# Attention and mixer: zero products around q's transposes, 1e-6 on TensorE, and a new order of the early loads

## The chip, the cores and the metric

The kernel runs on one core of a Trainium2 chip. Its time is the device time of one execution in microseconds, here the median over several runs. The engines of the core run side by side and each works through its own list of instructions in order: TensorE (PE) multiplies matrices, with weight loads shown apart as PEld; VectorE (DVE) and ScalarE (ACT) work element by element; GpSimd (POOL) casts, fills and issues transfers; SyncE (SP) issues transfers.

## The reference

Eight batches of eight heads, 576 positions, 64 features a head. First an attention without softmax, whose features are weighted by cosine and sine of the position; then a mixer on its output, laid out as x of 576 positions by 512 channels.

```python
theta = np.pi / 2.0 * pos / S
q_p = phi(q, cos_w, sin_w)          # [relu(q) * cos, relu(q) * sin]
k_p = phi(k, cos_w, sin_w)
kv = np.einsum('bhsf,bhsd->bhfd', k_p, v)
z = np.sum(k_p, axis=2)
num = np.einsum('bhsf,bhfd->bhsd', q_p, kv)
den = np.einsum('bhsf,bhf->bhs', q_p, z)[..., None] + 1e-06
x = num / den                       # heads side by side
h = x.transpose(0, 2, 1) @ U @ V    # U: 576 x 32, V: 32 x 576
u = x + h.transpose(0, 2, 1)
out = u + np.maximum(u @ w_ch1, 0.0) @ w_ch2   # 512 -> 2048 -> 512
```

## The kernel before

A batch's 576 positions are cut into four chunks of 128 rows and a tail of 64 (chunk number 4). Two batches make a pair, whose tails share one chunk. All matrix work is in bf16 with sums in fp32.

**The first batch** is done on its own and in a hurry. SP issues the loads of q, k and the second half of v's heads (the odd rows and the even rows apart: load_odd, load_even). POOL issues U and V, then v's first half of heads (load_v0, after cast_v's three casts), then the quarters of w_ch1 (w1_load: 512 of the 2048 columns each). PE meanwhile multiplies zeros (keep_warm: n products of 512 columns and `short` of 128), until q_prep has made a chunk's features; then it transposes q chunk by chunk, with one more zero product behind each. After four more zero products come spread_v (V's transposed layout), the z products of k, and kv0_mm, which needs v's first half. first_chain then carries batch 0 to the first products of the mixer: den_mm multiplies q by z, recip adds 1e-6 and takes the reciprocal on DVE, xh_mm and xh_norm make x, A_mm and the uTd functions make u transposed, and g_half begins the products with w_ch1.

**From there on** PE's order is written out as a list of slots. A slot is one piece of PE work of four matmuls or more: slots 0 to 15 are u times w_ch1 for batch 0 (g1_main, line 572, evicted by ACT at line 581), 16 to 31 the products with w_ch2 for batch 0 (g2_part, line 744; slots 16 to 19 use w_ch2's first quarter, the next four its second), and slot 32 begins batch 1's g1_main. Beside a slot, `at(j, ...)` hangs the small work of batch 1's attention: it is put into every engine's list just behind slot j. In the order of need these units are:

- q_prep and k_prep: for one chunk, the cosine half and the sine half, each on the engine named in the pair (DVE is V_, ACT is A_)
- qtr_unit: eight transposes of q on PE, evicted by DVE
- v_prep: a cast of one chunk of v for half of the heads
- kv_unit: k times v for half of the heads, 20 products (line 343)
- x_two and x_unit: x of one chunk, with 1e-6 and the reciprocal on DVE and the scaling on ACT or DVE
- A_unit, u_mm, u_add, utr_dma: the mixer's first part and the transposes by SP

The list of `at` is filled chunk by chunk in the order (4, 0, 1, 2, 3). So behind a slot that has several units, they stand in that order: at slot 12 of the kernel before, DVE's list has the casts of v's chunks 4, 0, 1 and 2, then k's chunk 3, then v's chunk 3.

**The queues.** A transfer is issued by the engine in whose list it stands, in order, when what it waits for is done. SP's list after batch 0's loads: q of batch 1 (line 94 and 88), k, then v in four pieces; after slot 15 a tiny transfer into `mark2` that waits for w_ch2's first quarter (the function gate, line 1240), the transposes of u of batch 0 (u_dma), a second gate for w_ch2's second quarter, and the loads of batch 2. POOL's list: after w_ch1's first two quarters a tiny copy into `mark` that waits for batch 0's k features, then the other two quarters; then a copy into `mark` that waits for batch 1's k (line 1227), and w_ch2's four quarters.

Of the kernel before, what the change touches and what calls it, by code (L numbers as in the profile page):

```python
# [11 lines left out]
BF16 = mybir.dt.bfloat16  # L12
# [5 lines left out]
def kernel(  # L18
# [22 lines left out]
    NJ = DH // P  # L41
    NPAIR = B // 2
    TS = 64

    def tail(b):
        lo = TS * (b % 2)  # L50
# [76 lines left out]
    def cast(eng, o, i):  # L127
        if eng is nc.scalar:
            nc.scalar.activation(out=o, in_=i, func=AF.Copy, bias=0.0, scale=1.0)
        else:  # L130
            eng.tensor_copy(out=o, in_=i)  # L131
# [89 lines left out]
    V_.memset(v_ext[:, 0:4, :, D:E], 1.0)  # L221
    V_.memset(q_tlT, 0.0)
    V_.memset(x_tl, 0.0)

    def keep_warm(n, tag, bufs, short=0):
        w_ps = ps.tile([P, 512], FP32, tag=tag, bufs=bufs, name="w_ps")
        for i in range(n + short):
            w = 512 if i < n else P
            nc.tensor.matmul(  # L229
                out=w_ps[:, 0:w], lhsT=zero[:, 0:P], rhs=zero[:, 0:w], start=True, stop=True  # L230
            )
# [11 lines left out]
        G_.memset(v_ext[:, 4 + i, :, :], 0.0)  # L243
        G_.memset(v_ext[tail(i), 4 + i, :, D:E], 1.0)

    def cast_v():
        nine_v = stV.rearrange("r (m k) -> r k m", k=9)
        for i in range(2):
            cast(
                G_,  # L250
                V_nat[:, 0:512].rearrange("r (c m i) -> r c m i", c=4, i=2)[:, :, :, i],
                nine_v[:, 5 * i : 5 * i + 4, :],
            )
        cast(G_, V_nat[:, 512:S], nine_v[:, 4, :])

    def cast_u():
        cast(G_, U_bf[:, 0:4, :], stU[:, 0:4, :])
# [149 lines left out]
    def recip(rec, den):  # L407
        nc.vector.tensor_scalar(out=rec, in0=den, scalar1=1e-6, scalar2=None, op0=ALU.add)
        nc.vector.reciprocal(out=rec, in_=rec)
# [641 lines left out]
    O2, G3 = ("o", 2), ("g", 3)  # L1051

    def den_mm(b, h0, h1, d_ps):
        for c in range(5):
            for h in range(h0, h1):
                nc.tensor.matmul(
                    out=d_ps[:, c, h - h0 : h - h0 + 1],
                    lhsT=qT_of(b, c, h),
                    rhs=z_sb[:, h : h + 1],
                    start=True,  # L1060
                    stop=True,
                )

    def xh_mm(b, c, h0, tag=None, bufs=None, acc=None):
# [48 lines left out]
    def first_chain(b):  # L1113
        v_block(b, 4, 8, 3, 4, A_)
        v_prep(b, 4, 8, (4,), (A_,))
        v_block(b, 4, 8, 0, 3, V_)
        cast(A_, z_sb, z_ps)
        cast(V_, kv_sb[b][:, 0:4, 0:D], kv_lo)
        spread_evac(A_)
        d0 = ps.tile([P, 2, 512], FP32, tag="X", bufs=1, name="d_ps")  # L1120
        d = [d0[:, i, 0:20].rearrange("p (c h) -> p c h", h=4) for i in range(2)]
        rec = [pool.tile([P, 5, 4], FP32, tag="rec5", bufs=2, name="rec5") for _ in (0, 1)]
        den_mm(b, 0, 4, d[0])
        recip(rec[0], d[0])
        x0 = [xh_mm(b, c, 0, *G3) for c in ORD[0:3]]
        for n in (0, 1):
            xh_norm(b, ORD[n], 0, rec[0], x0[n])
        kv_unit(b, 1, *O2, A_, D)
        for c, tg in zip(ORD[3:], (O2, T1)):
            x0.append(xh_mm(b, c, 0, *tg))  # L1130
        den_mm(b, 4, 8, d[1])
        xh_scale(b, ORD[3], 0, rec[0], x0[3])
        xh_norm(b, ORD[2], 0, rec[0], x0[2])
        recip(rec[1], d[1])
        xh_norm(b, ORD[4], 0, rec[0], x0[4])
        x1 = [xh_mm(b, c, 4, *G3) for c in ORD[0:2]]
        a_ps = ps.tile([P, DM], FP32, tag="o", bufs=2, name="a_ps")
        for _ in range(2):
            nc.tensor.matmul(out=a_ps, lhsT=zero[:, 0:P], rhs=zero, start=True, stop=True)
        x1.append(xh_mm(b, ORD[2], 4, *G3))  # L1140
        x34 = ps.tile([P, 2, 512], FP32, tag="X", bufs=1, name="x34_ps")
        for i in range(2):
            x1.append(x34[:, i, 0:256].rearrange("p (i d) -> p i d", d=D))
            xh_mm(b, ORD[3 + i], 4, acc=x1[-1])
        A_mm(b, a_ps, (0, 1))
        xh_scale(b, ORD[2], 4, rec[1], x1[2])
        for n in (0, 1):
            xh_norm(b, ORD[n], 4, rec[1], x1[n])
        cast(V_, A_of(b)[0:TS, :], a_ps[0:TS, 0:P])
        uT_alloc(b)  # L1150
        for i, (tag, bufs) in enumerate((T1, O2)):
            uT_ps[b, i] = ps.tile([P, 4, P], FP32, tag=tag, bufs=bufs, name="uT_ps")
            open_mm(b, i, uT_ps[b, i], range(4))
        for i in range(2):
            uTd_mm(b, i)
        uTd_evac(b, 0, A_)
        for n in (3, 4):
            xh_norm(b, ORD[n], 4, rec[1], x1[n])
        uTd_evac(b, 1, V_)
        A_mm(b, a_ps, (2, 3))  # L1160
        cast(A_, A_of(b)[TS:P, :], a_ps[TS:P, 0:P])
        u2 = ps.tile([P, 2, 512], FP32, tag="X", bufs=1, name="u2")
        uT_ps[b, 2] = u2[:, 0, :].rearrange("p (c t) -> p c t", c=4)
        uT_ps[b, 3] = ps.tile([P, 4, P], FP32, tag="T", bufs=1, name="uT_ps")
        for i in (2, 3):
            open_mm(b, i, uT_ps[b, i], range(4))
        for i in (2, 3):
            uTd_mm(b, i)
        uTd_evac(b, 2, V_)
        uTd_evac(b, 3, A_)  # L1170
        for d in range(2):
            g_half(b, d, range(3))
        for d in range(2):
            g_half(b, d, (3,), O2)

    FEATS = [(V_, V_ if c == 3 else A_) for c in TL]
    qT_alloc(0)
    keep_warm(4, "X", 1, 72)
    t_q = []
    for c in TL:  # L1180
        tg = G3 if c < 3 else O2
# [1 line left out]
    for c in TL:  # L1183
        q_prep(0, c, FEATS[c])
        qtr_mm(0, c, 0, H, t_q[c])
        keep_warm(1, "X", 1)
    for c, eng in zip(TL, (V_, A_, V_, A_, V_)):
        qtr_evac(0, c, eng, t_q[c])
    keep_warm(4, "X", 1)
    cast_v()  # L1190
    load_v0()
    for n in range(2):
        w1_load(n)
    cast_u()
# [24 lines left out]
    first_chain(0)  # L1219
    load_odd(qst, q, 1)  # L1220
    load_even(qst, q, 1)
    load_odd(kst, k, 1)
    load_even(kst, k, 1)
    for h0 in (0, 4):
        load_odd(vst, v, 1, h0, h0 + 4)
        load_even(vst, v, 1, h0, h0 + 4)
    G_.tensor_copy(out=mark, in_=kst[0:TS, 7, 4, 0:1])
    for n in range(4):
        w2_load(n)
    q_prep(1, 4, (V_, A_))  # L1230
    q_prep(1, 0, (V_, V_))


# [8 lines left out]
    for n, c in enumerate(ORD):  # L1242
        if n > 1:
            at(n - 2, lambda c=c: q_prep(1, c, (V_, V_)))
        tg = ("T", 1) if n % 2 else O2
        at((1, 2, 4, 5, 6)[n], lambda c=c, tg=tg: qtr_unit(1, c, eng=V_, tag=tg[0], bufs=tg[1]))
        at((6, 7, 9, 10, 12)[n], lambda c=c: k_prep(1, c, (V_, A_)))
        for i in range(2):
            at((12, 14)[i], lambda c=c, i=i: v_prep(1, 4 * i, 4 * i + 4, (c,), (V_,)))
    for hg in range(2):  # L1250
        at((14, 16)[hg], lambda hg=hg: kv_unit(1, hg, "T", 1))

    side = {}

# [33 lines left out]
                op=ALU.mult,  # L1288
            )

    for a, c in ((17, 0), (17, 4), (19, 1), (19, 2), (20, 3)):
        if c in (0, 2):
            at(a, lambda c=c: x_two(1, c))
        else:
            at(a, lambda c=c: x_unit(1, c, "X", 1))
# [190 lines left out]
```

## Time and profile before

| what | us |
|---|---|
| median of 3 runs (295.07 to 295.89) | 295.85 |
| the profiled execution | 295.75 |
| its span, from first to last instruction | 294.0 |
| PE busy | 288.3 |
| DVE busy | 205.7 |
| ACT busy | 161.7 |
| POOL busy | 51.0 |
| first transpose of q starts on PE | 8.94 |
| first product of kv0_mm starts | 16.16 |
| first product of den_mm starts | 17.17 |
| first product with w_ch1 starts | 23.18 |
| first product with w_ch2 starts (slot 16) | 40.44 |

Landings of the early transfers in that execution, from the issue to the last of the engines that carry it:

| transfer | issued | landed |
|---|---|---|
| k of batch 0, even rows | 3.06 | 12.10 |
| v of batch 0, first half, even rows | 8.37 | 16.11 |
| w_ch1, first and second quarter | 9.13, 9.87 | 20.47, 24.92 |
| q of batch 1, even rows | 10.21 | 23.83 |
| w_ch1, third and fourth quarter | 15.76, 16.50 | 30.86, 34.94 |
| k of batch 1, odd and even rows | 14.97, 15.68 | 28.09, 32.83 |
| v of batch 1, four pieces | 16.33 to 24.68 | 35.12 to 37.31 |
| w_ch2, four quarters | 33.41 to 35.83 | 39.93, 43.10, 45.95, 49.16 |

How to read it: a busy engine is not yet the bound, and a transfer that lands late costs only what an engine in PE's chain waits for it. The profile lists an engine's idle time in brackets with what ended it. The ends of matmuls are modelled; the steps from one end to the next are what PE's stream is read by.

### The profile page before, as it was taken

The numbers are of one execution on the slowest core, as the hardware profiler recorded it, in microseconds if no ns is written. First come the engines' busy times: TensorE is split into PE (matmuls) and PEld (weight loads), VectorE is DVE, ScalarE is ACT, GpSimd is POOL, SyncE is SP. The second block draws the span as 40 slices with busy tenths as digits, with TensorE's granted clock in tenths as the row PEclk, the third lists the DMA queues.
The fourth block names the chain that finished last, engine by engine and source line by source line (L and its number), as shares of the span: only waits on it lengthen the run. The fifth ranks groups of instructions, "written<-read, shape, count | busy, mean of one in ns | idle before, by whom it ended". The sixth has DMA issues, their size and how long they took to land.

```text
span 294.0 us, 7234 instructions
## 1 busy us (share of the span) xinstructions
PE 288.3 (98%) x2922; PEld 194.9 (66%) x2922; DVE 205.7 (70%) x497; ACT 161.7 (55%) x323; POOL 51.0 (17%) x89
## 2 busy tenths in 40 slices
PE   8999999999999999999999999999999999999995
PEld 6775454445745545676757666766776668889984
DVE  4878645696774569837736794678747798785864
ACT  2856654066791767568735865378752334446220
POOL 8520400012020002310500231021200100000240
PEclk9999999999999999999999999999999999999999
DMA  7999999999997998999599939992900141101013
GB/s 218 297 254 252 242 188 221 217 308 211 330 197 101 280 283 221 216 320 308 136 189 222 308 101 236 224 353 65 240 13 3 74 89 74 71 2 71 2 72 145
DMA packets 90709, 54.07 MB, mean 184 GB/s; under 512 B 58420, under 2 KB 87380, under 8 KB 90676
## 3 DMA queue, kind: packets, MB, share of 16 engines
q1 hardware_dynamic: 84116, 43.85, 59.7%
q0 software_dynamic: 6416, 9.63, 14.6%
q8 instruction: 23, 0.38, 0.5%
q10 hardware_dynamic: 144, 0.13, 0.1%
q14 instruction: 10, 0.08, 0.1%
HBM read 36.86 MB, written 9.44 MB: 157 GB/s over the span
## 4 chain that ended last, share of the span: by engine, by line
PE 89%; DMA 6%; ACT 2%; DVE 1%; issue 1%; DVEq 0%; ACTq 0%
PE g_ps L572 30%; PE h_ps L873 27%; PE o_ps L744 10%; DMA kst<-in_k_dram 6%; PE gt_ps L706 5%; PE c_ps L666 4%; PE kv_ps L343 3%; PE w_ps L229 3%; PE x_ps L418 3%; PE h_ps L744 1%; PE a_ps L441 1%; ACT k_p L302 1%; PE va_ps L471 1%; PE t_ps L373 1%; PE x_ps L1266 0%
## 5 line engine op out<-in xcount | busy, mean ns | idle before, releaser
L572 PE MATMUL g_ps<-uT,w_bf 128*128 128x512 bf16 x440 | 107.5, 379 | 0.1
L581 ACT ACTIVATE hid<-g_ps 128x512 bf16<-128x512 f32 x112 | 66.2, 599 | 72.3 <-PE g_ps L572 72.1
L572 PEld LDWEIGHTS <-w_bf 128*128 128x128 bf16 x440 | 41.3, 98 | 37.3 <-issue 0.8
L873 PEld LDWEIGHTS <-hid 128*128 128x128 bf16 x480 | 45.4, 98 | 9.6
L873 PE MATMUL h_ps<-w_bf,hid 128*128 128x256 bf16 x288 | 37.0, 273 | 0.0
L831 DVE TENSOR_TENSOR o_sb<-u_bf,h_ps 128x256 f32<-128x256 bf16 x44 | 18.3, 415 | 18.1 <-PE h_ps L873 17.9
L744 PE MATMUL o_ps<-w_bf,hid 128*128 128x512 bf16 x128 | 30.1, 379 | 0.0
L131 POOL CAST v_ext<-vst 128x512 bf16<-128x512 f32 (+1 forms) x26 | 18.5, 734 | 54.8 <-DMA vst<-in_v_dram 53.6
L873 PE MATMUL h_ps<-w_s,S 128*128 128x256 bf16 x208 | 26.5, 272 | 0.0
L873 PE MATMUL h_ps<-w_s,hid 128*128 128x256 bf16 x192 | 24.9, 273 | 0.0
L931 POOL DMA_DIRECT2D out_dram<-o_sb x16 | 10.0, 625 | 84.2 <-DVE o_sb L831 81.4
L479 DVE TENSOR_TENSOR u_bf<-x_bf,va_ps 128x512 bf16<-128x512 bf16 x27 | 17.7, 680 | 7.7 <-PE va_ps L471 5.4
L873 PEld LDWEIGHTS <-S 128*128 128x128 bf16 x208 | 19.9, 98 | 4.4
L831 DVE TENSOR_TENSOR o_sb<-o_sb,h_ps 128x256 f32<-128x256 f32 (+1 forms) x36 | 15.4, 430 | 10.4 <-PE h_ps L873 10.2
L744 PEld LDWEIGHTS <-hid 128*128 128x128 bf16 x128 | 11.6, 98 | 12.5
L706 PE MATMUL gt_ps<-uT_tl,w_bf 128*128 128x128 bf16 x256 | 16.1, 219 | 0.0
L428 DVE TENSOR_TENSOR x_bf<-x_ps,rec 128x512 bf16<-128x512 f32 x22 | 15.2, 691 | 0.8
L706 PEld LDWEIGHTS <-w_bf 128*128 128x128 bf16 x256 | 15.0, 98 | 1.0
L302 ACT ACTIVATE k_p<-kst,cosw 128x512 bf16<-128x512 f32 x20 | 14.2, 712 | 0.1
L302 ACT ACTIVATE q_p<-qst,sinw 128x512 bf16<-128x512 f32 x18 | 12.6, 709 | 1.9 <-DMA qst<-in_q_dram 1.9
L604 DVE TENSOR_TENSOR hid<-kept,c_ps 128x256 bf16<-128x256 f32 x24 | 9.4, 417 | 5.3 <-PE c_ps L666 2.8
L229 PE MATMUL w_ps<-zero 128*128 128x128 bf16 (+1 forms) x86 | 11.2, 301 | 1.2 <-DVE zero L140 1.2
(186 smaller groups left out, 419.5 us busy)
## 6 DMA issues: line engine op xcount, KB each, us to landing
qst<-in_q_dram SPq DMA_DIRECT2D x14, 512.0 KB, 6.0
kst<-in_k_dram SPq DMA_DIRECT2D x14, 512.0 KB, 6.4
vst<-in_v_dram SPq DMA_DIRECT2D x12, 512.0 KB, 6.7
out_dram<-o_sb POOLq DMA_DIRECT2D x19, 256.0 KB, 3.9
w_bf<-in_moe_w_ch_dram POOLq DMA_DIRECT2D x8, 512.0 KB, 12.3
out_dram<-o_sb SPq DMA_DIRECT2D x16, 256.0 KB, 2.8
qst<-in_q_dram SPq DMA_DIRECT2D x2, 640.0 KB, 13.6
kst<-in_k_dram SPq DMA_DIRECT2D x2, 640.0 KB, 9.0
```

The lines of the kernel that those rows point to most:

```text
L131: eng.tensor_copy(out=o, in_=i)
L229: nc.tensor.matmul(out=w_ps[:, 0:w], lhsT=zero[:, 0:P], rhs=zero[:, 0:w], start=True, stop=True)
L302: nc.scalar.activation(out=o, in_=i, func=AF.Relu, bias=0.0, scale=w)
L428: nc.vector.tensor_tensor(out=x_of(b, c, rows).rearrange("p (g i d) -> p g i d", g=2, d=D), in0=view[:, :, :, 0:D], in1=rec[rows].unsqueez ...
L479: nc.vector.tensor_tensor(out=u_bf[b][:, j, :, :], in0=x_bf[b][:, :, ns], in1=va[b][j].rearrange("p (c n) -> p c n", c=4), op=ALU.add,)
L572: nc.tensor.matmul(out=g_ps.rearrange("p (c t) -> p c t", c=4), lhsT=w1_bf[:, d, j * P : j * P + P], rhs=uT[b][:, d, :, :], start=(d == 0) ...
L581: nc.scalar.activation(out=hid[b][:, j, :], in_=g_ps, func=AF.Relu, bias=0.0, scale=1.0)
L666: nc.tensor.matmul(out=w[to].rearrange("p (c t) -> p c t", c=2), lhsT=lhs[:, d, cs], rhs=rhs[:, d], start=(first and d == 0), stop=(d == 1 ...
L706: nc.tensor.matmul(out=g_ps[:, jj, :], lhsT=w1_bf[:, d, j * P : j * P + P], rhs=uT_tl[pr][:, d, :], start=(d == 0), stop=(d == 3),)
L744: nc.tensor.matmul(out=o[:, cols], lhsT=lhs[:, j, c * P : c * P + P], rhs=w2_bf[:, j, cols], start=(j == 0), stop=(j == NJ - 1),)
L831: eng.tensor_tensor(out=o, in0=x, in1=y, op=ALU.add)
L873: nc.tensor.matmul(out=acc, lhsT=lhs[:, j, :], rhs=rhs[:, j, :], start=(j == 0 and at is not None), stop=(j == 7), skip_group_check=at is ...
```

## The change

Five edits, all before slot 24:

- keep_warm at the start: 4 products of 512 columns and 72 of 128 become 13 and 10; the one zero product behind each chunk's transposes goes (five in all); the four behind the evictions become eight.
- cast_v is cut in two: the first cast stands ahead of load_v0, the other two behind it.
- den_mm begins with two products of one row, of 20 columns each, that put 1e-6 into the whole bank (the sum of 9.98e-07 and 1.62e-09 in bf16, times 1); the den products then add to it, and first_chain takes the reciprocal without the add on DVE. Three memsets on DVE fill the operand. x_unit and x_two keep recip.
- SP's loads of batch 1's k and v stand behind a tiny transfer into mark2 that waits for w_ch1's second quarter. POOL's copy into mark, with w_ch2's loads behind it, waits no longer for batch 1's k but for batch 1's q features of chunk 1.
- The units of batch 1 come later: transposes of q from slots 1, 2, 4, 5, 6 to 4, 5, 7, 8, 9; k_prep from 6, 7, 9, 10, 12 to 11 to 15; v_prep from 12 and 14 to 14 and 15; kv_unit from 14 and 16 to 16 and 17; the x units from 17, 17, 19, 19, 20 to 18, 18, 20, 20, 21. The sine half of q's chunk 4 and of k's chunks 0 and 2 moves from ACT to DVE.

```diff
+    EPS = (9.98377799987793e-07, 1.622538547962904e-09, 1.0)
...
+    eps = pool.tile([1, 2 * P + 20], BF16, tag="S2", bufs=2, name="eps")
+    for cs, part in zip((slice(0, P), slice(P, 2 * P), slice(2 * P, None)), EPS):
+        V_.memset(eps[:, cs], part)
...
-    def cast_v():
+    def cast_v(i):
         nine_v = stV.rearrange("r (m k) -> r k m", k=9)
-        for i in range(2):
-            cast(
...
+        cast(
...
+        if i:
+            cast(G_, V_nat[:, 512:S], nine_v[:, 4, :])
...
     def den_mm(b, h0, h1, d_ps):
+        for i in range(2):
+            nc.tensor.matmul(
+                out=d_ps.rearrange("p c h -> p (c h)"), lhsT=eps[:, i * P : i * P + P],
+                rhs=eps[:, 2 * P :], start=(i == 0), stop=(i == 1),
+            )
...
-                    start=True,
+                    start=False,
                     stop=True,
+                    skip_group_check=True,
...
-        recip(rec[0], d[0])
+        V_.reciprocal(out=rec[0], in_=d[0])
...
-        recip(rec[1], d[1])
+        V_.reciprocal(out=rec[1], in_=d[1])
...
-    keep_warm(4, "X", 1, 72)
+    keep_warm(13, "X", 1, 10)
...
         qtr_mm(0, c, 0, H, t_q[c])
-        keep_warm(1, "X", 1)
...
-    keep_warm(4, "X", 1)
-    cast_v()
+    keep_warm(8, "X", 1)
+    cast_v(0)
     load_v0()
+    cast_v(1)
...
     load_even(qst, q, 1)
+    nc.sync.dma_start(out=mark2, in_=w1_bf[0:1, 0, 512:513])
     load_odd(kst, k, 1)
...
-    G_.tensor_copy(out=mark, in_=kst[0:TS, 7, 4, 0:1])
-    for n in range(4):
-        w2_load(n)
-    q_prep(1, 4, (V_, A_))
+    q_prep(1, 4, (V_, V_))
     q_prep(1, 0, (V_, V_))
...
-        at((1, 2, 4, 5, 6)[n], lambda c=c, tg=tg: qtr_unit(1, c, eng=V_, tag=tg[0], bufs=tg[1]))
-        at((6, 7, 9, 10, 12)[n], lambda c=c: k_prep(1, c, (V_, A_)))
+        at((4, 5, 7, 8, 9)[n], lambda c=c, tg=tg: qtr_unit(1, c, eng=V_, tag=tg[0], bufs=tg[1]))
+        at((11, 12, 13, 14, 15)[n], lambda c=c, n=n: k_prep(1, c, (V_, V_ if n % 2 else A_)))
         for i in range(2):
-            at((12, 14)[i], lambda c=c, i=i: v_prep(1, 4 * i, 4 * i + 4, (c,), (V_,)))
+            at((14, 15)[i], lambda c=c, i=i: v_prep(1, 4 * i, 4 * i + 4, (c,), (V_,)))
     for hg in range(2):
-        at((14, 16)[hg], lambda hg=hg: kv_unit(1, hg, "T", 1))
+        at((16, 17)[hg], lambda hg=hg: kv_unit(1, hg, "T", 1))
+
+    def w2_loads():
+        G_.tensor_copy(out=mark, in_=q_p[1][0:TS, 1, 7, 127:128])
+        for n in range(4):
+            w2_load(n)
+
+    at(3, w2_loads)
...
-    for a, c in ((17, 0), (17, 4), (19, 1), (19, 2), (20, 3)):
+    for a, c in ((18, 0), (18, 4), (20, 1), (20, 2), (21, 3)):
```

## The prediction

> **What bounds the kernel now.** I read the busy times by stage first, then the chain that ended last, then the DMA queues stage by stage, then the timeline around the changed lines. The columns of the first view are: window, its length, then busy us of PE, PEld, DVE, ACT and POOL with their instruction counts, the granted clock, the DMA share and GB/s.
>
> ```profile
> 16.20:23.20 7.00, 7.00 (x172) 5.68 (x173) 4.94 (x15) 3.78 (x14) 1.05 (x2) 1.00 1.16 254
> 34.00:41.00 7.00, 6.92 (x49) 3.28 (x47) 4.51 (x16) 6.33 (x13) 2.59 (x4) 1.00 0.97 150
> 50.00:290.00 240.00, 239.73 (x2350) 163.67 (x2349) 171.74 (x402) 131.75 (x254) 35.42 (x49) 1.00 0.69 175
> 293.80:294.10 0.30, 0.00 (x0) 0.00 (x0) 0.00 (x0) 0.00 (x0) 0.00 (x0) 0.64 0.00 0
> ```
>
> From 16 us on TensorE (PE) never rests, and after 50 us it is busy 239.73 of 240 us. So whatever this change does before 50 us is carried to the end unaltered: each us by which PE is earlier or later at 50 us is a us of the result. The chain of waits tells where the early stage loses time.
>
> ```profile
> 1.19 7.92 PE w_ps L229 x76
> ...
> 15.68 17.15 DMA kst<-in_k_dram
> ...
> 32.92 0.72 ACT k_tl L302
> ...
> 34.12 0.61 ACT k_p L302
> ...
> 35.27 3.70 PE g_ps L572 x16
> ```
>
> Columns: start, duration, what. Batch 1's k lands at 32.83 us; ScalarE (ACT) waits for it in front of evictions of g_ps, and PE then lacks a free bank. I take PE's losses as the steps between ends of successive matmuls beyond those of an undisturbed stream (215 ns for 512 columns): 0.12 us at 34.5, 0.24 at 35.7, 0.09 at 38.3 and 0.16 at 39.2, **0.61 us** in all.
>
> The DMA queues: q1 carries SP's loads, q0 POOL's (packets, MB, share). The first two lines are for 16 to 22 us, the next two for 30 to 33 us, the last for 37 to 43 us.
>
> ```profile
> q0 software_dynamic: 704, 0.69, 68.0%
> q1 hardware_dynamic: 707, 0.83, 46.9%
> ...
> q1 hardware_dynamic: 930, 1.01, 95.8%
> q0 software_dynamic: 76, 0.07, 13.5%
> ...
> q0 software_dynamic: 1101, 1.09, 115.0%
> ```
>
> With both queues loaded each gets the same number of packets, 118 per us; q1 nearly alone gets 310, q0 alone 184. This is the table on which the forecast hangs.
>
> **The front.** Before, the 76 zero products run from 1.19 until q's first transpose at 8.94. After: 13 of 512 columns at 0.427 us (the step of the first ones) end at 6.74, the ten short ones at about 7.5. q's first chunk is ready when ACT's 0.71 us from 7.08 is over, so the transposes begin near 7.85. Then they go at the pace of q_prep (ACT 0.65 us a chunk; the last piece on VectorE (DVE) ends at 10.14) and end near 10.7, instead of 12.2. Eight products of 0.216 us follow (four before), to 12.4, and spread_v to 12.8. The first z product then waits for k, whose second half lands at 12.10: 12.1 + 0.71 = 12.8, against 13.78 before. But the next bound is v's first half:
>
> ```profile
> 7.72 0.66 POOL L156 DMA_DIRECT2D v<-in_v_dram  x1
> 8.37 0.77 POOL L160 DMA_DIRECT2D v<-in_v_dram  x1
> ...
> 16.15 0.41 PEld L1101 LDWEIGHTS <-k_p 128*128 128x128 bf16 x12 [0.84 <-DMA v<-in_v_dram]
> ```
>
> It lands at 16.11 and PE has idled 0.84 us for it. Two of the three casts (1.64 us together) move behind its issue; the one left takes about 0.7, so the load goes out 0.9 us sooner. All of that reaches PE only if the transfer keeps its speed. It will now run beside q1's last k and v packets, so k may land up to about 0.5 us later. Bounds 0 to 0.9; I take **-0.75**.
>
> The eps products: no one-row matmul is in the trace. Four of 20 columns at the 25 to 29 ns step of the smallest ones give +0.11 at least. The nearest row is spread_v's 32-row pair at 13.43: its first product comes 0.10 us late, and so does the first 128-row product behind it (0.08 to 0.11, here and at each of the 32-row products of u). Two excursions so priced are 2 x (0.21 + 0.05) = **+0.50**, which I take. The two removed DVE adds (0.18 us each) save nothing on PE, since PE is busy 7.00 of 7.00 us in that stretch; had PE been waiting for rec, they would have paid 0.4. The Trainium skill, TensorEngine Tiling, Key Properties, says that changing the tiling mode drains the array; it states it for modes and gives no price. By it the one-row product would be the dear one, without it the cheap one, -0.39 to the sum. The three memsets of eps lie in DVE's idle time (2.65 us) before q lands. Front: -0.75 + 0.50 = **-0.25** (-0.8 to +0.5).
>
> **ACT's part.** Units and engines move so that k is needed from slot 11, not slot 6, two sin halves of k and one of q go to DVE, and PE keeps its banks: **-0.6** (0 to -0.61). DVE gets 3 x 0.48 us more, in 10.8 us in which it is busy 7.9.
>
> **The held loads.** SP now stops at mark2 until w_ch1's second quarter has landed: 24.9 us before, perhaps 24.4. Behind it on SP's queue stand all six k and v loads of batch 1, then the gate on w2, batch 0's transposes back and batch 2's loads. mark2 costs 0.7, the first issue 0.6, and the first packets come 1.5 us after (as at the start of the program): 26.6 us. Before, k's packets followed q's at once, at 23. In the same step w2's loads move ahead on POOL. Before:
>
> ```profile
> 32.95 0.18 POOL L1227 COPY mark<-kst 64x1 f32<-64x1 f32 x1 [15.70 <-DMA kst<-in_k_dram]
> 33.41 3.18 POOL L123 DMA_DIRECT2D w_bf<-in_moe_w_ch_dram  x4 [0.28 <-issue]
> ```
>
> Now POOL's mark waits for q_p of chunk 1 only, made by DVE after q lands at 23.83: six halves at 0.39 us, 26.3; w2 is issued from 26.6 and its packets flow from about 28.8. So batch 1's k and v, 2048 packets, run beside the rest of w1 and beside w2's 2048 packets, where before their second half ran alone. At 118 per us throughout they need 17.4 us and land at 44.0. If w1's rest ends on most engines before w2 begins, up to 2 us go at 310: 3.3 us less, 40.8. Landing is set by the last of the 16 engines (v's last load landed on them between 33.5 and 37.3 us), so I stay near the late end: **43.4** for v's last load, where it was 37.31.
>
> What waits for it:
>
> ```profile
> 37.42 0.28 DVE L131 CAST v_tl<-vst 128x256 bf16<-128x256 f32 x1
> 37.62 0.89 DVE L131 CAST v_ext<-vst 128x256 bf16<-128x256 f32 x4
> ```
>
> At slot 15 DVE's queue holds four casts of v's second half (0.22 us apart) and behind them the cos half of k's chunk 3, which kv_unit(1, 0) after slot 16 needs. So kv_unit starts at landing + 0.1 + 0.88 + 0.47 + 0.2 = landing + 1.65 = 45.05. PE would be there at: 40.44 (slot 16 before) - 0.60 (the first kv unit, moved behind it) - 0.61 (stalls gone) + 0.86 (slot 16) - 0.25 (front) = 39.85. PE stands still for **+5.2 us**: 2.6 if v lands at 40.8, 5.8 at 44.0. w2's first quarter, needed at slot 16, is no limit: it follows w1 on q0.
>
> **The x units** move by one slot, A_unit stays at 22:
>
> ```profile
> 47.84 0.94 ACT L1276 ACTIVATE x_bf<-side,rec 128x64 bf16<-128x64 f32 x4
> 48.81 0.29 PEld L441 LDWEIGHTS <-U_bf 128*32 128x32 bf16 x20 [0.42 <-issue]
> ```
>
> ACT ends x_bf at 48.78 and PE's A products start at 48.81, so there is no slack. x_two(1, 2) to the end of ACT's scaling takes 3.5 us from 45.27; with one slot (0.86) fewer between, PE arrives 2.9 us after: **+0.6** (0 to 0.9). u's transposes still land before slot 32, since both move together (0.9 us of slack before).
>
> Sum: -0.25 - 0.6 + 5.2 + 0.6 = +4.95 on the profiled execution's 295.75 (span 294.0): **300.7**; the median of the runs, 295.85, is 0.1 above it.
>
> **Rivals.**
>
> 1. *v is in time* (the other side). If v lands by 38.2, nothing stalls there: 295.75 - 0.5 - 0.6 = 294.65, with the eps products at half price and the x units covered. For it: q1 alone moves 310 packets per us, and 2048 of them need 6.6 us. Against it: POOL's queue is never empty from 28.8 on. The point from which it decides is the landing at 38.2.
> 2. *A short stall*, landing near 40: 1.8 us, 297.3. For it: most engines run ahead of the last one by up to 3.8 us, and that one may lag less when q1 is let in later.
> 3. *The stall also costs the clock.* At the end of the program the granted clock is 0.64 in the last 0.3 us, some 3.2 us after the last matmul; and the first matmuls step at 0.427 us, not 0.215, until 7.16 us. A PE that stands for 5 us may come back at half speed and stay so for up to 6 us, as at the start: +1.5 to 3, so 303. The Trainium skill, TensorE: Matmul & The Clock Gate, Why this matters for your kernels, asks for no idle gap of PE over some 3 us; no gap inside this trace tests it. The same rule bears on q's transposes, which lose their fillers; their pauses are 0.2 us each, and the row of this trace has none so long as to decide.
>
> That the change does not do what it says (w2 still waits for k) would need POOL's mark to come late; nothing on POOL stands before it.
>
> **Chances.** Forecast (298.5 to 302.5): 0.50. Clock rival (302.5 to 305): 0.18. Short stall (295.5 to 298.5): 0.12. In time (294 to 295.5): 0.20. A measurement of this kernel tells about 0.3%, 0.9 us, from no change. Faster by more than that is rival 1 but for its upper edge, 0.18; the same is that edge and the lower part of the short stall, 0.07; slower 0.75. The range reaches from 294.5 in rival 1 to 303.7 in rival 3, leaving out a little of both; the forecast's own range is 298.5 to 302.5.
>
> **What would show it.** Right: kst issued near 25 on SP; q0 and q1 with equal packets from 29 to 40; vst's last landing after 41; PE idle before kv_ps L343 for several us; PE at d_ps 0.2 us or more sooner than 17.17; steps of 0.1 us at the eps products. Wrong: v landed by 38.2 or w2 issued after 33, PE without a gap around 40 us, or a granted clock that falls after q's transposes.

## The result and the profile after

| | before | changed |
|---|---|---|
| median of 6 runs, us | 295.73 (295.07 to 297.13) | 298.90 (298.44 to 303.36) |
| ratio, with its 95% interval | | 1.0106 (1.0074 to 1.0139) |
| the profiled execution, us | 295.75 | 298.47 |
| its span, us | 294.0 | 296.7 |
| first transpose of q, its end | 9.16 | 8.13 |
| first product of the first den_mm, end | 17.33 | 17.01 |
| last den product, end | 19.52 | 20.25 |
| first product with w_ch1, end | 23.57 | 24.30 |
| first product of slot 16, end | 40.81 | 40.34 |
| first product of u (u_mm of batch 1), end | 50.40 | 52.86 |
| k of batch 1, odd rows landed | 28.09 | 30.54 |
| v of batch 1, last piece landed | 37.31 | 41.01 |

The changed kernel is slower by about 1%. In some executions of every kernel here, among them the slowest of these six (303.36), the granted clock of PE falls to half for one or two stretches of 3.4 us, and the ratios leave the most disturbed executions out, so a median and a ratio need not agree.

First the busy times by stage of the changed kernel (window, length, busy us of PE, PEld, DVE, ACT and POOL with counts, granted clock, DMA share, GB/s):

```profile
16.20:23.20 7.00, 5.94 (x141) 4.93 (x141) 4.59 (x14) 3.76 (x15) 0.54 (x1) 1.00 1.17 252
34.00:41.00 7.00, 7.00 (x42) 3.42 (x40) 4.45 (x13) 5.41 (x10) 0.00 (x0) 1.00 1.21 224
39.50:43.00 3.50, 2.04 (x26) 1.20 (x24) 1.50 (x6) 1.84 (x4) 0.00 (x0) 1.00 1.23 205
50.00:290.00 240.00, 239.53 (x2352) 162.38 (x2350) 171.95 (x401) 133.44 (x262) 37.23 (x49) 1.00 0.67 170
```

PE stands still in two places where it did not before: for 1.06 us between 16.2 and 23.2, and for 1.46 around 41. Of the 1.06 us, 0.40 lie ahead of the first den_mm, where PE waits for ACT's z_sb (in the kernel before PE stood 0.54 us at 15.6, outside this window), and 0.66 in the second den_mm. Behind 50 it is as busy as it was. The chain that ended last names both (start, duration, what):

```profile
4.41 11.37 DMA vst<-in_v_dram
...
19.36 0.66 issue
...
28.12 12.89 DMA vst<-in_v_dram
...
41.11 0.30 DVE v_tl L128
41.40 0.61 DVE v_ext L128 x3
42.01 0.40 DVE k_p L304
...
42.55 0.67 PE kv_ps L343 x17
```

Where before the chain ran over k's landing and ACT, it now runs over v's last piece, DVE's four casts and the cos half of k's chunk 3 into kv_unit. The same place in the timeline (in brackets: idle before, and what ended it):

```profile
41.11 0.30 DVE L128 CAST v_tl<-vst 128x256 bf16<-128x256 f32 x1 [2.04 <-DMA vst<-in_v_dram]
41.31 0.69 DVE L128 CAST v_ext<-vst 128x256 bf16<-128x256 f32 x3
41.92 0.48 DVE L304 TENSOR_SCALAR k_p<-kst,cosw 128x512 bf16<-128x512 f32 x1
...
42.55 0.19 PE L343 MATMUL kv_ps<-v_ext,k_p 128*128 128x65 bf16 x1 [1.46 <-DVE k_p L304]
```

kv_unit has done three products when it meets k's chunk 3; its end then jumps from 41.09 to 42.74, **1.63 us** beyond the stream. The new loss in the front is in the second den_mm:

```profile
18.64 0.21 PE L1055 MATMUL d_ps<-eps 1*128 1x20 bf16 x2
18.78 0.55 PE L1061 MATMUL d_ps<-z_sb,q_pT 128*128 128x1 bf16 x16
...
19.20 0.16 PE L1061 MATMUL d_ps<-z_sb,q_tlT 128*128 128x1 bf16 x1
20.02 0.14 PEld L1061 LDWEIGHTS <-q_tlT 128*128 128x128 bf16 x3 [0.75 <-issue]
20.02 0.23 PE L1061 MATMUL d_ps<-z_sb,q_tlT 128*128 128x1 bf16 x3 [0.66 <-issue]
```

Seventeen products go in a row, and the last three come **0.81 us** later though all their operands have long been there; the idle time is put down to "issue", a wait for nothing that the profile shows. w_ch2's loads, which stood behind the landing of kst before, in the timeline of POOL:

```profile
27.21 0.30 POOL L1258 CAST mark<-q_p 64x1 f32<-64x1 bf16 x1 [10.47 <-DVE q_p L304]
27.66 3.13 POOL L120 DMA_DIRECT2D w_bf<-in_moe_w_ch_dram  x4
```

And the two queues from 27 to 32 us, from 32 to 37 and from 37 to 41.1 (packets, MB, share):

```profile
q1 hardware_dynamic: 1522, 1.68, 95.6%
q0 software_dynamic: 91, 0.09, 10.4%
...
q0 software_dynamic: 629, 0.63, 75.5%
q1 hardware_dynamic: 530, 0.58, 40.7%
...
q0 software_dynamic: 809, 0.81, 118.3%
q1 hardware_dynamic: 56, 0.06, 5.0%
```

w_ch2 is issued from 27.66, but its packets come only from 32.0. Until then k and v have the engines almost alone; from then on v's last two pieces share them, and v's last 56 packets take from 37 to 41.

### The profile page after: what moved, and what is told of

It is laid out like the page before. It is cut to its first block, busy times and chain, and to the rows that moved or that the text cites. A ratio compares the mean times of both kernels' runs of the same rounds, so it can differ in the third digit from the quotient of the medians.

```text
span 296.7 us, 7134 instructions
## 1 busy us (share of the span) xinstructions
PE 287.0 (97%) x2872; PEld 191.1 (64%) x2872; DVE 207.5 (70%) x501; ACT 160.0 (54%) x320; POOL 53.1 (18%) x89
## 4 chain that ended last, share of the span: by engine, by line
PE 85%; DMA 8%; DVE 3%; ACT 2%; issue 1%; DVEq 0%; ACTq 0%
PE g_ps L572 28%; PE h_ps L873 26%; PE o_ps L744 10%; DMA vst<-in_v_dram 8%; PE gt_ps L706 5%; PE c_ps L666 4%; PE kv_ps L343 3%; PE x_ps L418 2%; PE h_ps L744 1%; PE a_ps L441 1%; PE va_ps L471 1%; ACT hid L581 1%; PE g_ps L589 1%; ACT x_bf L1287 1%; PE d_ps L1061 0%
## 5 line engine op out<-in xcount | busy, mean ns | idle before, releaser
L128 POOL CAST v_ext<-vst 128x512 bf16<-128x512 f32 (+1 forms) x26 | 20.3, 805 | 56.3 <-DMA vst<-in_v_dram 53.7
L304 DVE TENSOR_SCALAR k_p<-kst,sinw 128x512 bf16<-128x512 f32 x25 | 13.3, 536 | 0.0
L343 PEld LDWEIGHTS <-k_p 128*128 128x128 bf16 x240 | 10.6, 97 | 4.2 <-issue 1.6
```

The source lines that it names most:

```text
L304: eng.tensor_scalar(out=o, in0=i, scalar1=0.0, scalar2=w, op0=ALU.max, op1=ALU.mult)
L343: nc.tensor.matmul(out=acc[:, i, :], lhsT=k_of(b, c, h), rhs=v_tl[:, h, 0:n] if c == 4 and b < 2 else vx[:, c if c < 4 else 4 + b % 2, h, ...
```

## The experiments

The theories. **T (sharing)**: the early w_ch2 delays v, and v's last piece costs PE 1.6 us at kv_unit; A waits 0.6 more since the x units stand one slot later. **P (pause)**: the pause in the second den_mm comes with the short list of zero products. The rivals to these: DVE's order rather than the landing makes kv_unit late; the hold at mark2 is what delays v; and what the front loses, 0.73 us, comes from v0 or from the 1e-6 on PE.

| kernel | median, us (runs) | before beside it | ratio (95%) |
|---|---|---|---|
| e1 | 298.65 (6) | 295.89 | 1.0123 (1.0084 to 1.0162) |
| e2 | 298.72 (6) | 295.89 | 1.0097 (1.0077 to 1.0118) |
| e3 | 297.30 (10) | 295.89 | 1.0051 (1.0024 to 1.0077) |
| e4 | 299.11 (6) | 295.89 | 1.0116 (1.0085 to 1.0147) |
| e5 | 300.13 (12) | 296.15 | 1.0059 (1.0018 to 1.0101) |
| e6 | 297.04 (12) | 296.15 | 1.0036 (0.9998 to 1.0074) |
| e7 | 296.63 (12) | 296.15 | 1.0026 (0.9995 to 1.0057) |
| e8 | 295.91 (12) | 296.15 | 0.9982 (0.9951 to 1.0012) |
| e9 | 299.95 (6) | 296.19 | 1.0106 (1.0058 to 1.0154) |
| e10 | 296.32 (12) | 296.19 | 1.0008 (0.9978 to 1.0037) |
| e11 | 295.30 (12) | 296.19 | 0.9964 (0.9936 to 0.9992) |

Diffs are against the changed kernel unless another is named.

**e1: k's chunk 3 ahead of v's casts on DVE.**

```diff
-        at((11, 12, 13, 14, 15)[n], ... k_prep(1, c, (V_, V_ if n % 2 else A_)))
+        at((11, 12, 13, 14, 14)[n], ... k_prep(1, c, (V_, A_ if n in (0, 2) else V_)))
```

> The changed kernel, with k's chunk 3 prepared behind slot 14 and wholly on DVE, so that it no longer stands behind the casts of v's second half; no transfer is touched. Theory (PE stands 1.63 us before kv_unit because DVE's list puts k's chunk 3 behind v's last load): the load still lands near 41.0, the gap before kv_ps L343 goes, slot 17 runs in its place, and the time falls by 1.6 us from 298.9 to 297.3. Rival (the gap is the transfers' own doing and only moves to the second kv unit): the gap reappears before kv_unit(1, 1) with 1 us or more and the time stays at 298.5 or above.

kv_unit's first half no longer waits, though v's last piece lands at 41.28. The wait moves to its second half:

```profile
41.37 0.30 DVE L128 CAST v_tl<-vst 128x256 bf16<-128x256 f32 x1 [1.75 <-DMA vst<-in_v_dram]
41.58 0.90 DVE L128 CAST v_ext<-vst 128x256 bf16<-128x256 f32 x4
42.39 0.42 DVE L128 CAST kv<-kv_ps 128x260 bf16<-128x260 f32 x1
...
42.86 0.28 PE L343 MATMUL kv_ps<-v_ext,k_p 128*128 128x65 bf16 x4 [0.64 <-DVE kv L128]
```

The step there is 0.8 us too long. So about half of the 1.63 us comes from k's chunk 3 standing on DVE behind casts that wait for v. The other half is DVE's list again: the eviction of kv's first half (42.39) stands behind v's five casts, and PE waits for it. v's casts alone end at 42.48, 0.25 us behind the product ahead of the gap (42.23), so v's landing costs what it does mainly by way of what stands behind it on DVE. u comes 1.06 us sooner (51.80), the profiled execution takes 297.49 against 298.47; the medians, 298.65 and 298.90, are too close for their spread to show it. In the trace the outcome lies between the theory (no gap left) and the rival (1 us or more); the 297.3 that the theory named did not come.

**e2: w_ch2 behind k again.**

```diff
-        G_.tensor_copy(out=mark, in_=q_p[1][0:TS, 1, 7, 127:128])
+        G_.tensor_copy(out=mark, in_=kst[0:TS, 7, 4, 0:1])
```

> The changed kernel, with POOL's mark waiting for batch 1's k again, so that w_ch2 is issued after k has landed (about 32.5 us) and not at 27.7. Theory (v is late because w_ch2 shares the DMA engines with it): v's last load lands at 36 to 38, not 41.0, the gap of 1.63 us before kv_unit goes, and the time falls to 297.3; w_ch2's first quarter lands near 39.5, just ahead of slot 16. Rival (v is late because it is held behind w_ch1): v still lands at 40 or later and the time stays at 298.5 to 299.5, or slot 16 waits for w_ch2 and it grows.

w_ch2 is issued at 32.58; v's last piece lands at 35.03 instead of 41.01, and slot 16 does not wait for w_ch2's first quarter (landed 38.53). In kv_unit 0.5 us are left, for another unit of the same slots: the sin half of k's chunk 3 on ACT.

```profile
41.73 0.20 PE L343 MATMUL kv_ps<-v_ext,k_p 128*128 128x65 bf16 x1 [0.34 <-ACT k_p L302]
```

T holds for the landing. Of the 1.1 us that kv_unit gains in this pair of profiles, a longer pause in den_mm, 1.25 us, takes 0.3 back, and u comes 0.79 us sooner (52.07). The median, 298.72, does not show the gain, and the expected 297.3 did not come; four of the six executions lost the clock (a mean below 0.998).

**e3: the zero products as they were.**

```diff
-    keep_warm(13, "X", 1, 10)
+    keep_warm(4, "X", 1, 72)
...
         qtr_mm(0, c, 0, H, t_q[c])
+        keep_warm(1, "X", 1)
...
-    keep_warm(8, "X", 1)
+    keep_warm(4, "X", 1)
```

> The changed kernel with the zero products of the kernel before (4 and 72, one behind each chunk's transposes, four behind the evictions). Theory (the 0.75 us in which PE stands inside the second den_mm, released by nothing that the trace shows, is PE's list of instructions being fetched late, because 100 instructions fewer come before it): the pause goes, q's transposes start 1 us later without delaying k or v, and g_ps begins 0.5 to 0.8 us sooner; 298.9 falls to about 298.2. Rival (the pause belongs to the eps products or to den_mm itself): it stays, and the front is as late as in the changed kernel or later, 298.9 to 299.6.

The second den_mm of this kernel in its timeline:

```profile
18.50 0.20 PE L1055 MATMUL d_ps<-eps 1*128 1x20 bf16 x2
18.64 0.55 PE L1061 MATMUL d_ps<-z_sb,q_pT 128*128 128x1 bf16 x16
19.05 0.24 PE L1061 MATMUL d_ps<-z_sb,q_tlT 128*128 128x1 bf16 x4
```

The last four follow in step. The first product with w_ch1 ends at 23.34, 0.23 us ahead of the kernel before and 0.96 ahead of the changed one; the ratio falls from 1.0106 to 1.0051. v's last piece lands at 39.45 here and kv_unit loses 1.03 us instead of 1.63. How much of that reaches the end is another matter: kv_unit is bound by v here too. Its waiting product starts at 40.99 instead of 42.55, 1.56 us sooner, and v's last piece landed at 39.45 instead of 41.01, 1.56 sooner. Whether the zero products have a part in that landing was not settled: in the six kernels with the hold and an early w_ch2 it goes from 38.20 to 42.11, and mostly with the pace of all early loads in that execution (k of batch 0 landed at 10.79 where v came at 38.20, at 11.54 in e3, at 12.30 where v came at 42.11; e1, with k at 11.63 and v at 41.28, does not fit this order). What the short list costs without this cover is read from e7 against e2.

**e4: v0 issued behind all three casts.**

```diff
     cast_v(0)
-    load_v0()
     cast_v(1)
+    load_v0()
```

> The changed kernel with v's first half issued behind all three casts again. Theory (the sooner issue only exchanges places with the other half of v: it landed at 15.79 instead of 14.34): the second half lands near 14.4, the first near 16.1, and den_mm starts within 0.4 us of the changed kernel's 16.71, so the time stays within 0.4 us of 298.9. Rival (the sooner issue is a gain of its own): den_mm starts 0.7 us or more later and the time is 299.6.

In this execution all early transfers land about 1.4 us sooner (k 10.79, v0 13.82), so the start of den_mm, 15.71, says nothing of v0. Measured from k's landing, v0 comes 3.0 us later (2.7 in the changed kernel, 4.0 before) and v's second half 1.5 (3.6 and 2.2): v0 and v's second half exchange places, which fits but rests on one execution. The pause is there, 1.33 us. Inconclusive on v0.

**e5: the short list, with 54 one-column zero products behind it.**

```diff
     keep_warm(13, "X", 1, 10)
+    pad_ps = ps.tile([P, 512], FP32, tag="X", bufs=1, name="pad_ps")
+    for _ in range(54):
+        nc.tensor.matmul(
+            out=pad_ps[:, 0:1], lhsT=zero[:, 0:P], rhs=zero[:, 0:1], start=True, stop=True
+        )
```

> The changed kernel with 54 zero products of one column behind its opening zero products, so that PE's list is as long as with the old zeros, while the wide products are those of the changed kernel and q's transposes start as soon as q allows. Theory (the pause in the second den_mm is PE's list fetched late because it is 100 instructions shorter there): the pause of 0.8 to 1.3 us, present in all four profiles with the short list and absent in the two with the long one, goes, and g_ps begins at 23.2 to 23.6, as with the old zeros; the time is near that of the old zeros, 297.3. Rival (the pause comes with the sparse transposes, whatever the length of the list): it stays, g_ps begins at 24.0 or later, 298.5 or more.

No pause; w_ch1's first product ends at 23.16 (its record is missing, and is set in one step of 0.32 us behind the product ahead of it, as in the other kernels). Refilling the list is enough to remove the pause, then, without the old products or the fillers between the transposes. But the median is far off: in half of the twelve executions the clock fell; the other six have a median of 297.16, close to the 297.01 of e3's executions that kept theirs. In the profiled one v lands at 42.11, PE stands from 39.94 to 43.64, and the clock is at half from 41.97 to 48.80.

**e6: e3, and 1e-6 added by DVE again** (the eps tile and its memsets go too).

```diff
     def den_mm(b, h0, h1, d_ps):
-        for i in range(2):
-            nc.tensor.matmul(... lhsT=eps[:, i * P : i * P + P], ...)
...
-                    start=False,
+                    start=True,
...
-        V_.reciprocal(out=rec[0], in_=d[0])
+        recip(rec[0], d[0])
```

> The changed kernel with the old zero products and with 1e-6 added by DVE again, no eps products. To be held against the run with the old zeros alone. Theory (the eps products cost PE 0.22 us each time, and DVE's add is hidden because PE does not wait for rec): g_ps begins 0.4 us sooner than 23.34 after den_mm's first product, relative to that product, and the time falls by 0.3 to 0.5. Rival (the add lies on the path): no difference or later by up to 0.4.

From the first den product to the last it takes 2.18 us, against 2.43 in e3: 0.25 us for the pair of one-row products between them. With both pairs gone, w_ch1's first product ends 0.47 us sooner (22.87, set in as in e5, against 23.34). In the executions that kept their clock the medians are 296.39 and, in e3, 297.01.

**e7: e3 and e2 together** (both diffs above).

> The changed kernel with the old zero products and with w_ch2 issued behind batch 1's k: two undone together. Theory (the two losses are separate: 0.9 us in the front, and the gap before kv_unit, 1.06 us with the old zeros): v lands near 35, the gap falls to the 0.5 us that ACT's half of k's chunk 3 costs, and the time is 0.5 us below the old zeros' alone, 296.8. Rival (w_ch2 then comes late and slot 16 or 20 waits): 297.3 or more, with a gap at o_ps.

v lands at 34.54, kv_unit loses 0.52, A still waits; w_ch1's first product ends at 23.09 (set in as in e5). Against e3 the ratio is 1.0026 to 1.0051; the intervals overlap, and the 0.6 us in the executions that kept their clock (296.4 and 297.0) is about what the waits at kv_unit differ by (1.03 less 0.52). The two profiled executions do not show it (297.40 here, 296.93 in e3): in this one PE stands for another 1.18 us at 159 us, where no edit reaches. Against e2 only the zero products differ, and v is in time in both: w_ch1's first product ends 1.5 us sooner (24.61 in e2, with its pause of 1.25), u still comes 1.5 us sooner (50.55 against 52.07), and the ratio goes from 1.0097 to 1.0026, with intervals that do not meet. So with v's wait gone the short list costs its whole pause of 1.3 us; the ratios differ by more, since four of e2's six executions lost the clock and two of e7's twelve.

**e8: e7 with batch 1's units sooner.**

```diff
-        at((11, 12, 13, 14, 15)[n], ... k_prep(...))
+        at((8, 9, 10, 11, 12)[n], ... k_prep(...))
...
-            at((14, 15)[i], ... v_prep(...))
+            at((12, 13)[i], ... v_prep(...))
...
-        at((16, 17)[hg], ... kv_unit(...))
+        at((14, 16)[hg], ... kv_unit(...))
...
-    for a, c in ((18, 0), (18, 4), (20, 1), (20, 2), (21, 3)):
+    for a, c in ((17, 0), (17, 4), (19, 1), (19, 2), (20, 3)):
```

> As the one before it, and the units of batch 1 nearer to where they were: k from slot 8 to 12, v at 12 and 13, kv_unit at 14 and 16, the x units at their old slots; q's transposes stay at 4 to 9 and DVE keeps the sine halves. Theory (with k and v landing by 35, what is left of the loss is the wait for k's chunk 3, 0.5 us, and that of A_unit for ACT, 0.7 us): both go, PE runs without a gap from 24 to 50 us, and the time is 295.2, 0.5 to 0.7 below the kernel before. Rival (the early units wait for k again, as in the kernel before): gaps of 0.3 to 0.6 us at g_ps from 33 on, 295.9 or more.

kv_unit and A wait for nothing; from slot 16 to u 9.59 us pass, as before the change. 295.91 against e7's 296.63 beside it.

**e9: e3 without the hold**, w_ch2 early.

```diff
     load_even(qst, q, 1)
-    nc.sync.dma_start(out=mark2, in_=w1_bf[0:1, 0, 512:513])
     load_odd(kst, k, 1)
```

> The changed kernel with the old zero products and without the transfer into mark2, so that batch 1's k and v follow q at once; w_ch2 stays early. To be held against the old zeros alone, where v's last load landed at 39.45 and PE stood 1.06 us before kv_unit. Theory (w_ch2's early issue makes v late, and the hold adds to it by starting k 4 us later): k flows beside w_ch1 from 23 on, v's last load lands at 37 to 38.5, the gap before kv_unit is 0.5 us or less, and the time falls by 0.5 to 296.7. Rival (the hold helps, since w_ch1 and then k and v each have the engines alone): v lands at 39.5 or later, the gap is 1 us or more, 297.3 or above.

The queues from 27 to 32 us, and kv_unit:

```profile
q1 hardware_dynamic: 904, 1.05, 64.4%
q0 software_dynamic: 421, 0.41, 49.0%
```

```profile
41.98 0.30 DVE L128 CAST v_tl<-vst 128x256 bf16<-128x256 f32 x1 [2.65 <-DMA vst<-in_v_dram]
...
43.42 0.21 PE L343 MATMUL kv_ps<-v_ext,k_p 128*128 128x65 bf16 x1 [3.62 <-DVE k_p L304]
```

Without the hold w_ch1's rest is spread among k and v (q0 moves 421 packets in these 5 us, not 91), and v's last piece lands at 41.89: no sooner than with the hold. So the rival that blamed the hold falls. That the hold helps is likely from the medians (299.95 here, 297.30 in e3) but not settled: 41.89 lies within the spread of e3's kind, and the intervals of the ratios overlap. With w_ch2 behind k the landings point the same way: 34.54 to 36.07 in the four kernels with the hold (e2, e7, e8, e11), 36.44 and 37.31 in the two without it (e10 and the kernel before), which differ in more than the hold. What v owes to the early w_ch2 is clear of that spread: at most 37.31 in these six, 38.20 to 42.11 in the seven with an early one.

**e10: the kernel before with only the new zero products** (against the kernel before).

```diff
-    keep_warm(4, "X", 1, 72)
+    keep_warm(13, "X", 1, 10)
...
         qtr_mm(0, c, 0, H, t_q[c])
-        keep_warm(1, "X", 1)
...
-    keep_warm(4, "X", 1)
+    keep_warm(8, "X", 1)
```

> The kernel before with the changed kernel's zero products alone (13 and 10, none behind the transposes, eight at the end). Theory (the shorter list of PE is what costs in the front): a pause of 0.7 to 1.3 us, released by nothing that the trace shows, stands between 17 and 21 us; g_ps begins at 23.6 to 24.5 although the transposes start 0.7 us or more sooner; more executions lose the clock for a window (granted clock 0.994 or less); 296.5 to 297.5. Rival (the zeros are a gain that other parts gave back): g_ps begins at 23.2 or sooner, 295.5 or less.

No difference in time (1.0008) and no pause in the profiled den_mm. This does not settle P, though. In the profiled execution the clock is at half from 16.51 to 19.92, and PE takes 2.82 us from the first den product to the last, not 2.19 as before: it comes to the place of the pause later than the kernels that had one. The six executions that kept their clock were not profiled; their median, 295.92, against 296.10 of eighteen of the kernel before that kept theirs (one of 1675 left out), leaves no room for a loss of 0.8 to 1.3 us in most of them. What the short list does cost here is clock: six of the twelve executions lost it, as expected, and four of the 23 of the kernel before beside them. q's first transpose ends 1.0 us sooner here (8.12) and nothing comes of it: v0 lands at 16.30, and PE does not go on with kv0_mm from 15.40 to 16.35.

**e11: e8, and 1e-6 added by DVE** (the diffs of e8 and e6 together).

> Old zeros, w_ch2 behind k, early units, and 1e-6 added by DVE again: what is left of the change is the hold of k and v, the sooner issue of v's first half, the later transposes of q and the sine halves on DVE. Theory (the eps products cost PE 0.22 to 0.26 us each time): 0.4 us below the kernel with the early units alone, 295.3 among executions that keep the clock, 0.5 us below the kernel before. Rival (front bound by the landing of k and v, in which the eps products are hidden): 295.7 or more.

The changed kernel's held loads and sooner v0, without its zeros, its eps products, its early w_ch2 and most of its later units (q's transposes stay at their new slots, and the sine halves on DVE). Busy times of 16.20 to 23.20 and of 24 to 50:

```profile
16.20:23.20 7.00, 7.00 (x149) 5.21 (x147) 5.51 (x16) 4.01 (x14) 0.17 (x1) 1.00 1.17 252
...
24.00:50.00 26.00, 25.74 (x250) 14.02 (x248) 18.38 (x53) 14.61 (x36) 3.37 (x5) 1.00 1.15 233
```

PE lacks nothing in the front and 0.26 of 26 us behind it; w_ch1's first product ends at 22.50, 1.07 us sooner than before. **Ratio 0.9964 (0.9936 to 0.9992): it beats both kernels**, by a little.

The steps side by side, as the ratios to the kernel before go: changed 1.0106, old zeros 1.0051, w_ch2 behind k 1.0026, units sooner 0.9982, DVE adds 0.9964. Single steps lie within each other's intervals; the whole way does not.

## Why the prediction was right, and where its terms were off

It said 300.7 (298.5 to 302.5 for its own case), slower, by a stall of PE at kv_unit; it is 298.9, slower, with that stall in that place. The mechanism holds, its size does not, and a front that was to gain has lost. The number is right with some luck. With the landing that came, 41.01, the prediction's own sum has a stall of 41.01 + 1.65 - 39.85 = 2.8 us and gives 295.75 - 0.25 - 0.6 + 2.8 + 0.6 = 298.3, below its range, and two of the six runs (298.44, 298.47) lie below it too.

| term | forecast | measured |
|---|---|---|
| v0 and the transposes | -0.75 | -0.41 |
| eps products | +0.50 | +0.34 |
| pause in den_mm | none | +0.81 |
| ACT's stalls gone | -0.6 | -0.6 |
| kv_unit | +5.2 | +1.6 |
| A later | +0.6 | +0.7 |
| behind u, in small steps | 0 | +0.3 |
| in all | +4.95 | +2.7 |

- **The queue term was mis-sized.** The step that was off is "w2 is issued from 26.6 and its packets flow from about 28.8", with "up to 2 us go at 310" for k and v. The issue came at 27.66, and the first packets not 2.2 but 4.3 us behind it. k and v moved 1522 packets in the 5 us from 27 to 32, and v landed at 41.01, near the early bound of 40.8. That it came so near the bound is luck, since two errors offset each other. By the prediction's own count, 5 us alone instead of 2 leave some 500 of the 2048 packets at 32, a little over 4 us at 118 per us, and v would have landed between 36 and 37. But the landing waits for the last of the engines that carry it: the 56 packets left at 37 took until 41, the last of them one by one, 0.14 us apart, while w_ch2 moved 809.

  The same showed in the front: load_v0 is issued 1.0 us sooner (6.70, not 7.72), and its packets begin near 11 us in both kernels, when SP's queue lets up. A load of POOL's starts slowly here while SP's queue runs at 300 packets per us, though both share evenly once it flows (629 and 530 packets from 32 to 37); why was not tried. The Trainium skill, DMA: Bandwidth & Descriptors, SWDGE vs HWDGE vs iDMA, has each engine take the queues in turn, which the even share from 32 to 37 bears out and the start does not.

  The step behind the landing was right: PE was to start at landing + 1.65, and does at + 1.54. The stall is 3.6 us shorter than said: 2.4 of it is the landing (43.4 against 41.01), 0.1 the shorter queue behind it, 1.0 is that PE arrives at kv_unit at 40.83, not 39.85, since its front lost 0.73 instead of gaining 0.25, and 0.1 the three products that were done. In the changed kernel itself, then, v's landing sets the end and the front's loss is covered by the wait for it: the sum adds up, but the two terms are not to be had apart.
- **The front.** The working holds, but for the pause and one reading: the 0.84 us that PE was said to have idled for v0 are those of its weight loads, its products stood for 0.54. The first den product ends 0.32 us sooner. PE stood idle ahead of the first eps pair until z_sb was done (16.66), and the first den product ends 0.35 us behind z_sb, against 0.26 before: this pair cost 0.09, and v0 and the transposes gained 0.41. v0 landed 1.17 sooner (14.94), but v's second half 1.45 later (15.79), and ACT's cast of it, at 15.87, stands ahead of z_sb. e4 fits this exchange without proving it. A pair of one-row products in a busy stream costs what was taken for it (0.25: e6, and the second pair here), not the cheap end, and DVE's two adds saved nothing, as PE's full stretch had said. Without the pause, in e3, the front is -0.69 + 0.22 + 0.24 = -0.23, where -0.75 + 0.50 = -0.25 was said; and that with the old zeros, so the sooner transposes give nothing.
- **The pause** was foreseen by no row; the prediction gave it no term. It is there in four kernels of four with the short list and the rest of the change (0.81 to 1.33 us: changed, e1, e2, e4), each time ahead of the same product, and in none with the old list (e3, e6 to e9, e11) or the padded one (e5), nor in e10. The traces make a late fetch of PE's list likely. The queue q8 carries instructions in packets of 16 KB, 22 in the five kernels with the short list and 23 in all others, and one of them goes from 17.70 to 18.64 in the changed kernel (view of 17.69 to 18.65):

```profile
q8 instruction: 1, 0.02, 6.1%
```

  In the four kernels such a packet ends 0.2 to 0.7 us ahead of the pause (18.64, 18.27, 19.00, 18.01), and PE goes on 1.3 to 1.5 us behind its end (20.02, 19.79, 20.33, 19.55). With the old list or the padded one the packet has ended by 14.9, and the next one starts when den_mm is done. In e10 it ends at 18.84, and PE, slowed by the half clock, comes to the same product 1.9 us later and does not wait. So e10 does not speak against a fetch; but why PE should go on 1.3 us and more behind a packet is not shown, and no run moved the packet alone: the cause is argued, not shown.
- **ACT's stalls** went as said: PE is busy 7.00 of 7.00 us from 34 to 41, and slot 16 comes at 40.81 + 0.73 - 0.60 - 0.61 = 40.33 (40.34 measured).
- **A** waits as said, and e8, with the x units in their old slots, has it gone.
- **Rivals.** v in time (by 38.2) did not happen, but e2 and e7 make it so, and e11, which undoes the zeros, the eps products and the units too, is 0.4% faster than before, near the 1.1 us that this rival named. The stall itself, 1.6 us, is that of the rival of a short stall (1.8); the time is above that rival's 297.3 mainly because the front, pause included, lost 0.73 where the rival's sum has it gain 0.25. The clock rival is not the profiled execution, but three of the changed kernel's six runs have it (298.91, 299.99, 303.36, mean clock 0.994 to 0.989), one of them (303.36) beyond the forecast's own range.

## What to carry to other kernels

A transfer moved ahead in one queue is paid by whatever shares the engines behind it: before moving a load earlier, ask which consumer is nearest to its landing, and keep the far one (w_ch2, needed 10 us later) behind the near one. When two transfers are due at the same step, bringing the one forward may only exchange them, as v0 and v's second half seem to have done here. Filler work that looks idle may carry something else: here removing it gained nothing (e10) and, with the other edits, cost a pause of 1.3 us (e2 against e7); try such an edit by itself before it goes in with others. And where a transfer's landing is set by the last of many engines, its mean rate does not tell when it lands.

## What the runs showed of the hardware that had not been expected

- **The clock falls after much shorter pauses than 3 us.** In e4's profile PE is busy 2.24 of the 3.41 us ahead of the fall (16.56 to 19.97), with no pause over 1.33, and then (window, length, busy us of PE, PEld, DVE, ACT and POOL, clock at 0.50, DMA share, GB/s):

```profile
20.00:23.40 3.40, 3.40 (x36) 2.16 (x32) 1.97 (x7) 0.93 (x4) 0.00 (x0) 0.50 1.20 253
```

  The same holds in e8 (busy 2.75 of the 3.41 us up to 16.25) and e10 (2.35 up to 16.51). But e1 and e2, with pauses nearly as long as e4's (1.16 and 1.25 us), kept their clock in the profiled execution, so the pause alone does not decide. The stretches at half clock last 3.41 us or 6.83 (16.25 to 23.08 in e8's profile, 43.13 to 46.54 in e9's, from near the end of a pause of 3.6). The Trainium skill, TensorE: Matmul & The Clock Gate, Part 1, has a free-running window of 3413 ns, and an idle one of these throttles; the lengths and e9 agree, while e4, e8 and e10 show that a window need not be idle, only thin. With the short list 22 of 36 executions lost clock (changed kernel, e1, e2, e4, e10), with the old list 13 of 64 (e3, e6, e7, e8, e9, e11) and 9 of 73 of the kernel before, where lost means a mean clock below 0.998. In e6 it is 5 of 12 and in e5, padded, 6, so the list is not the only cause: e5 and e9 lose it at kv_unit, e8 in the front after v0 came late.
- **A one-row product among 128-row ones costs 0.11 us at each side**, four times the step of a small product: in the changed kernel's second den_mm the ends lie 0.11, 0.03 and 0.11 us apart (18.71, 18.82, 18.85, 18.96), and e6 gives 0.25 us for the pair.
